# Two linear-attention blocks on one core: the turned strip of G goes by GpSimd's queue, and the kv products stand later

## The chip, the cores and the metric

The kernel runs on one core of a Trainium2 chip, as one program. Its engines each run an in-order queue: TensorE (PE) multiplies, VectorE (DVE) and ScalarE (ACT) do the elementwise work and empty PSUM, GpSimd (POOL) and SyncE (SP) issue DMAs. The metric is device time in microseconds: 573.85 us for the kernel before, the median of three runs (573.29 to 576.09).

## The reference

Two independent linear-attention blocks, A and B, each with its own x (1, 2048, 640), wqkv (640, 1920) and wo (640, 640), all float32; their outputs stand side by side in a (1, 2048, 1280) result. Per block, with 32 heads of 20:

```
q, k, v = split(x @ wqkv)                       # 32 heads x 20
phi(t)  = where(t > 0, t + 1, exp(t)) + 1e-6
kv  = sum over s of phi(k)[s] v[s]^T            # 20 x 20 per head
z   = sum over s of phi(k)[s]
o   = phi(q) kv / (phi(q) . z + 1e-6)
out = concat over heads(o) @ wo
```

## The kernel before

**Algebra.** The kernel never forms v. It sums G = X^T phi(K), a 640 x 640 matrix, over the rows of x, and gets kv = Wv^T G per head. kv is then multiplied with wo into a matrix M (640 x 640) that takes phi(q) straight to the output. Block A is "block one" (b=0), block B "block two" (b=1). Nearly every product is written as three matmuls of a high and a low part (names ending in h and l; DVE makes the low part by a subtraction, ACT the high part by a copy).

**Stages.** First come the k products and G of both blocks, then the q and o stages. Rows go in pairs of 128-row tiles (`kpair`, NPB = 8 pairs per block); a pair has seven k steps, each of 6 or 9 matmuls of 320 columns into a PSUM bank ka, kb or ke (L316). Into the steps of a pair `fill` puts other work: parts of G of the rows before (`gsteps`, L544; psg for 512 direct columns), and in pair NPB+1 block one's kv products (`kvmm`, L603).

**The turned strip.** G lives in one tile, `gall`, called gacc in the profile: 128 partitions x 5 x 640. Its columns 0 to 511 are computed directly. Its last 128 columns are computed transposed, as psr, and added into `gall[:, :, 512:]` (L557). When the sum is complete `gback` turns them: DVE transposes blocks of 32 x 32 into a tile gt (L579), four DMAs write it to DRAM as rd (L583; each 32 partitions x 20 pieces of 128 bytes, 80 KB), and one DMA reads the whole strip back into gall (L586; 320 KB, 640 pieces of 512 bytes). Before this read lands no kv product may start, since each reads all of G. This happens twice, once per block; both use gall.

**What sets the order.** Everything up to the start of the q stage is noted in a plan and emitted by a list scheduler: each job has an engine, a cost, a due time worked back from its users, and `dma` gives the share of the wire that it is taken to need. `safe` makes the planner count a DMA's result as later by up to so much, `late` sets how far behind PE's place a job without users may be due. PE's order is that of the notes; ACT, DVE, POOL and SP take what is due first, and SP has at most eight DMAs in flight in the plan. The queues that result are fixed in the program.

The q and o stages are written out by hand: a step ("q", u, c, k) is three matmuls of 512 columns into psq (L980 to L982), five of them (k = 0 to 4) for one of five column tiles c of a row group u; `at(slot, f, ...)` hangs further work on a slot, and `run(slot)` issues it. At the slot's place each f issues its whole work on all engines. So for block two `kvmm2` issues one group's kv products (L1040; ten matmul records), the mask on DVE (kvt, L1044) and the copy kvh on ACT; the subtraction kvl follows at the next slot. `load_o` loads wo (L1030), `split_o` splits it (woh on ACT, L974; wol on DVE, L971), `mmm2` multiplies kv and wo into psm. There are six groups of heads, four of six heads and two of four. kv uses the two PSUM banks tagged "e", and mmm2 takes one of these as well, so a third kv product waits until DVE has taken the first from its bank. `load_xraw` (L1011) loads the next group's rows of x, xql (L932) their stored low parts. After each column tile ACT computes eq and rq from psq (L1151, L1152) and DVE pq and acc (L1153, L1163).

**SP's queue** holds nearly all loads, the xd stores, and the rd and gacc transfers of the strip. **GpSimd's queue** holds the zacc transfers (sums of phi(k), L407), the small zd and zq transfers (L652, L654), and later stores.

Of the kernel before, what the change touches and what calls it, by code (L numbers as in the profile page):

```python
# [77 lines left out]
class Plan:  # L78
# [9 lines left out]
    def note(self, engine, n, fn, w, r, ahead=None, dma=None, late=None, by=None, due=None, safe=0.0, lat=0.0):  # L88
        base = self.RATE.get(engine)
        j = Job(engine, base[0] + base[1] * n if base else n, fn, ahead, dma)  # L90
        for part, writes in [(p, True) for p in w] + [(p, False) for p in r]:
            sp = part.space
            if sp.where is not None and sp not in j.spaces:
                j.spaces.append(sp)
            for lo, hi, other, wrote in sp.uses:
                if lo < part.hi and part.lo < hi and (writes or wrote) and other is not j:
                    j.deps.add(other)
            if writes:
                sp.uses = [u for u in sp.uses if not (part.lo <= u[0] and u[1] <= part.hi and u[2] is not j)]
            sp.uses.append((part.lo, part.hi, j, writes))  # L100
        for d in j.deps:
            d.nexts.append(j)
        for sp in j.spaces:
            sp.left += 1
        if engine == "PE":
            j.ideal = self.pe_at
            self.pe_at += j.cost
        j.late = self.pe_at + (25.0 if late is None else late)
        if by is not None:
            j.late = self.pe_at + by  # L110
        j.by, j.set, j.safe, j.lat = by, due, safe, (LAT if due is None else 1.9) + lat
        self.jobs.append(j)
        return j
# [105 lines left out]
def tile_linear_attn_pair(ctx: ExitStack, tc: tile.TileContext, ins, out: bass.AP):  # L219
    nc = tc.nc  # L220
    P = 128
# [3 lines left out]
    NG = NT // 4  # L225
# [5 lines left out]
    NPB = NT // 2  # L231
# [34 lines left out]
    gall = base.tile([P, NC, D], F32, name="gacc", tag="gacc", bufs=1)  # L266
# [15 lines left out]
    note = plan.note  # L282
# [29 lines left out]
    def mms(terms, o, start):  # L312
        n = len(terms)
        for k, ((ah, al), (wh, wl)) in enumerate(terms):
            for i, (a, w) in enumerate(((ah, wh), (ah, wl), (al, wh))):
                nc.tensor.matmul(o, a.r, w.r, start=start and k == i == 0,  # L316
                                 stop=k == n - 1 and i == 2, skip_group_check=True)
# [21 lines left out]
    rd = [dram.tile([D, P], F32, name=f"rd{b}") for b in range(NB)]  # L339
# [61 lines left out]
    def pk_split(hi, lo, p, n):  # L401
        note("ACT", n + 110, lambda: act(hi.r, p.f, AF.Identity, bias=epst), [hi], [p, K0.all], by=8.0)  # L402
        note("DVE", n, lambda: stt(lo.r, p.f, EPS, hi.f, op0=OP.add, op1=OP.subtract), [lo], [p, hi], by=9.0)  # L403
# [5 lines left out]
    def z_open(b):  # L409
        zac[b] = [Space("zacc", D, (GD,)) for _ in range(2)]  # L410

    def pk_space():
        return Space("pkh", D, GRP, F32R), Space("pkl", D, GRP, F32R)
# [53 lines left out]
    def kpair(p, fill):  # L467

        b = p // NPB
        first = p % NPB == 0  # L470
        if first:
            z_open(b)
        terms = kterms(kleft(p), wf[b])
        T = [Space("kt", D, ANY) for _ in range(2)]
        E = [Space("ek", D, ANY) for _ in range(2)]
        hl = [pk_space() for _ in range(2)]

        def step(n):
            tm, k, start = terms[n]
            rd = [x for a, w in tm for x in (*a, *w)]  # L480

            def products():
                o = BK[k].open(("ka", "ke", "kb")[k]) if start else BK[k].tile
                mms(tm, o[:, :HF], start)

            note("PE", MM * 3 * len(tm), products, [BK[k].all], rd)

        def copy(h, t, k):
            o = T[t][h * HF:h * HF + HF]
            note("ACT", HF, lambda: act(o.f, BK[k].tile[:, :HF], AF.Copy), [o], [BK[k].all])  # L490

        def plus(h, t, k):
            o = T[t][h * HF:h * HF + HF]
            note("DVE", HF, lambda: tt(o.f, BK[k].tile[:, :HF], o.f, op=OP.add), [o], [BK[k].all, o])

        def finish(n):
            e, t = E[n].all, T[n].all
            note("ACT", D, lambda: act(e.f, t.f, AF.Exp), [e], [t], by=6.0)
            note("ACT", D, lambda: act(t.f, t.f, AF.Relu), [t], [t], by=6.0)  # L499
            note("DVE", D, lambda: stt(e.f, e.f, 1.0, t.f, op0=OP.min, op1=OP.add), [e], [e, t], by=7.0)  # L500
            pk_split(hl[n][0].all, hl[n][1].all, e, D)
            z_add(first, zac[b][n].all, e)

        after = {0: [(copy, 0, 0, 0)], 2: [(copy, 1, 0, 0)], 3: [(plus, 0, 0, 2)], 4: [(copy, 1, 1, 0), (plus, 1, 1, 1)],
                 5: [(copy, 0, 1, 0), (finish, 1)], 6: [(plus, 1, 0, 1), (finish, 0)]}
        for n in range(7):
            step(n)
            for f, *a in after.get(n, ()):
                f(*a)
            for f, *a in fill.get(n, ()):  # L510
                f(*a)
        for t in range(2):
            pks[2 * p + t] = hl[t]
# [3 lines left out]
    WD = 4 * P  # L517
# [44 lines left out]
    def gsteps(i, s, alone=False):  # L562
        if s == 0:
            x, y, u = gset(i, True, 0, 2), gset(i, True, 2, 3), gset(i, False, 0)
            v = gset(i, False, 1, k=6 if alone else None)
            if alone:
                back = [(gback, i // NG)] if i % NG == NG - 1 else []
                return {0: [x[0], y[0], u[0], v[0], *x[1:], *y[1:], *u[1:], *back, *v[1:]]}
            out = {1: [x[0], y[0]], 3: [*x[1:], *y[1:]], 4: u, 5: [v[0]], 6: v[1:]}
        else:  # L570
            x, y, z = (gset(i, False, c) for c in (2, 3, 4))
            out = {1: [x[0]], 3: x[1:], 4: y, 5: [z[0]], 6: z[1:]}
        return out

    def gback(b):

        t = Space("gt32", D, ANY)
        turned = [G[b, c][WD:D] for c in range(NC)]
        note("DVE", D, lambda: nc.vector.transpose(t.all.f, gall[:, :, WD:]), [t.all], turned)  # L579
        rows = rd[b].rearrange("(j r) n -> r j n", r=32)  # L580
        v = Space("rd", 4)
        for q in range(4):
            note("SP", 0.07, lambda q=q: nc.sync.dma_start(  # L583
                rows[:, :, 32 * q:32 * q + 32], t.all.f[32 * q:32 * q + 32].rearrange("r (j s) -> r j s", s=32)),
                [v[q:q + 1]], [t.all], dma=0.6)
        note("SP", 0.07, lambda: nc.sync.dma_start(gall[:, :, WD:], rd[b].rearrange("(c p) n -> p c n", p=P)),  # L586
             turned, [v.all], dma=1.0, safe=6.0)

    kvt = {}

# [248 lines left out]
    def filled(i, s, late=False):  # L839
        fill = {}  # L840
        for n, x in gsteps(i, s).items():
            fill.setdefault(LATER[n] if late else n, []).extend(x)
        return fill
# [13 lines left out]
    gready(NG - 1)  # L857
    whole(NG - 1, 0)
    wf[1] = forms("wk", ins[1]["wk"], w_split)
    kpair(NPB, filled(NG - 1, 1))  # L860
    place = ((1, 6, 0, 6), (2, 0, 1, 6), (2, 2, 2, 6), (3, 0, 3, 6), (3, 2, 4, 6), (4, 0, 5, 6))
    kvs = {3: [(kvmm, g, (6, 7, 3)[g]) for g in range(3)], 4: [(kvmm, g, (4, 5, 6)[g - 3]) for g in range(3, 6)]}
    for p in range(NPB + 1, NP):
        if p == NPB + 1:
            fl = kvs
# [120 lines left out]
    def at(slot, f, *a):  # L986
        todo.setdefault(slot, []).append((f, a))
# [371 lines left out]

    for g in range(NGR):  # L1360
        at(("q", 0, 0, 0), load_o, 1, g)
        at(("q", 0, (0, 1, 1, 2, 2, 3)[g], (2, 0, 3, 0, 3, 0)[g]), kvmm2, 1, g)
        at(("q", 0, 1 + g, 1) if g < 4 else ("q", 1, 0, 2 * g - 7), split_o, 1, g)
        at((("q", 0, 2, 2), ("q", 0, 3, 2), ("q", 0, 4, 4), ("q", 0, 4, 4), ("q", 1, 1, 2), ("q", 1, 2, 2))[g], mmm2, 1, g)
        at((("q", 0, 2, 4), ("q", 0, 3, 4), ("q", 1, 0, 1), ("q", 1, 0, 3), ("q", 1, 1, 4), ("q", 1, 2, 4))[g],
           store_m, nc.gpsimd)

# [19 lines left out]
        at(("o", h - 1, 2 * c + 1), split_w, "q", 1, c)  # L1387

    for c in range(NC):
        at(("q", 0, (0, 0, 1, 1, 2)[c], (1, 4, 1, 4, 1)[c]), load_xraw, 1, c)  # L1390
        at(("q", 0, 4, c - 1) if c else ("q", 0, 3, 3), load_xq, 1, c)
        at(("q", 0, 4, c) if c else ("q", 0, 3, 4), round_xq, 1, c)
        for u in range(1, NU - 1):
            at(("q", u, 3, c), load_xraw, u + 1, c)
            at(("q", u, 4, c), load_xq, u + 1, c)
            at(("o", u - 1, 9 if (u, c) == (1, 2) else 2 * c + 4), round_xq, u + 1, c)
# [94 lines left out]
```

## Time and profile before

| what | value |
|---|---|
| time, median of three runs | 573.85 us (573.29 to 576.09) |
| the profiled execution's own time | 573.23 us |
| its span (first to last instruction) | 571.5 us |
| granted TensorE clock, mean | 0.997 |
| busy PE / DVE / ACT / POOL | 561.5 / 427.4 / 361.8 / 62.9 us |
| DMA | 118.92 MB, mean 208 GB/s over the span |

A wait is read as "engine, what, line <- releaser, tensor: us in total, times, longest". A row of the timeline gives start, length, engine, line, operation, output <- inputs, sizes and, in square brackets, the idle time of the engine before it and who ended it. On SP and POOL the length of a DMA row is the time that the engine needed to issue it; the list of DMAs gives the time from issue to landing. In rows of stretches stand the stretch, its length, then the busy time and count of PE, PEld, DVE, ACT and POOL, the granted clock, the share of the 16 DMA engines and GB/s.

### The profile page before, as it was taken

How to read it: one execution, taken by the hardware profiler on the slowest of the kernel's cores; microseconds unless marked ns; L12 is line 12 of the kernel's file. 1: busy time of each engine (PE TensorE's matmuls, PEld its weight loads, DVE VectorE, ACT ScalarE, POOL GpSimd, SP SyncE). 2: the span in 40 equal slices, each digit the busy share in tenths (PEclk: the TensorE clock that was granted, in tenths of full speed). 3: DMA queues.
4: the chain of work that ended last, by engine and by line, in shares of the span. 5: the costliest groups of instructions: out<-in, count | busy, mean ns of one | idle time of the engine just before them, and what ended most of it. 6: DMA issues, size and time to landing. Idle time of an engine off the chain costs nothing.

```text
span 571.5 us, 8956 instructions
## 1 busy us (share of the span) xinstructions
PE 561.5 (98%) x3224; PEld 512.3 (90%) x3224; DVE 427.4 (75%) x689; ACT 361.8 (63%) x668; POOL 62.9 (11%) x103
## 2 busy tenths in 40 slices
PE   9999999999999999999979999999999999999997
PEld 7998999988899999998858889898989989898997
DVE  7788687589888668987635799967788685767791
ACT  6777466574768757767225768675767656665551
POOL 0210011110011021111010102210012201001010
PEclk9999999999999999999989999999999999999999
DMA  8993755949939677798998994764273997122022
GB/s 307 379 256 116 201 146 138 269 102 280 295 100 249 189 194 214 209 288 230 276 326 281 324 322 150 257 229 137 90 256 110 340 392 272 47 75 92 1 93 92
DMA packets 74879, 118.92 MB, mean 208 GB/s; under 512 B 12084, under 2 KB 36692, under 8 KB 74836
## 3 DMA queue, kind: packets, MB, share of 16 engines
q1 hardware_dynamic: 65620, 91.05, 49.4%
q0 software_dynamic: 8928, 26.92, 16.9%
q8 instruction: 25, 0.41, 0.3%
q10 hardware_dynamic: 288, 0.39, 0.2%
q14 instruction: 18, 0.15, 0.1%
HBM read 71.78 MB, written 36.07 MB: 189 GB/s over the span
## 4 chain that ended last, share of the span: by engine, by line
PE 94%; DMA 2%; DVE 1%; SPq 1%; ACT 0%; issue 0%
PE psg L544 16%; PE pa L1293 12%; PE ka L316 9%; PE psq L980 8%; PE psq L982 8%; PE psq L981 8%; PE pe L1293 6%; PE psr L544 5%; PE ke L316 5%; PE psk L778 4%; PE psb L1293 4%; PE kb L316 3%; DMA gacc<-rd 2%; PE pskv L1040 1%; PE pskv L603 1%; PE psm L630 1%
## 5 line engine op out<-in xcount | busy, mean ns | idle before, releaser
L981 PE MATMUL psq<-xql,wh 128*128 128x512 f32 x200 | 78.2, 391 | 0.6 <-DMA xql<-xd 0.6
L980 PE MATMUL psq<-xqh,wh 128*128 128x512 f32 x200 | 78.7, 394 | 0.0
L982 PE MATMUL psq<-xqh,wl 128*128 128x512 f32 x200 | 78.2, 391 | 0.0
L544 PE MATMUL psg<-pkh,xnl 128*128 128x512 f32 x160 | 63.0, 394 | 0.0
L544 PE MATMUL psg<-pkl,xnh 128*128 128x512 f32 x160 | 62.8, 393 | 0.0
L544 PE MATMUL psg<-pkh,xnh 128*128 128x512 f32 x160 | 62.3, 389 | 0.0
L490 ACT ACTIVATE kt<-ka 128x320 f32<-128x320 f32 x52 | 22.7, 436 | 58.3 <-PE ka L316 58.0
L407 POOL DMA_DIRECT2D zacc<-ek x32 | 26.6, 830 | 229.8 <-DVE ek L500 168.0
L1153 DVE SCALAR_TENSOR_TENSOR pq<-eq,rq 128x512 f32<-128x512 f32 x40 | 27.6, 691 | 31.4 <-ACT rq L1152 31.3
L1151 ACT ACTIVATE eq<-psq 128x512 f32<-128x512 f32 x40 | 23.9, 597 | 37.5 <-PE psq L982 35.2
L981 PEld LDWEIGHTS psq<-xql,wh 128*128 128x128 f32 x200 | 37.7, 189 | 8.3 <-DMA xql<-xd 1.1
L982 PEld LDWEIGHTS psq<-xqh,wl 128*128 128x128 f32 x200 | 37.7, 188 | 8.0
L1308 ACT ACTIVATE o<-pa 128x320 f32<-128x320 f32 x64 | 27.9, 437 | 26.5 <-PE pa L1293 26.0
L980 PEld LDWEIGHTS psq<-xqh,wh 128*128 128x128 f32 x200 | 37.9, 189 | 7.2
L544 PEld LDWEIGHTS psg<-pkh,xnl 128*128 128x128 f32 x160 | 30.0, 188 | 6.4
L544 PEld LDWEIGHTS psg<-pkl,xnh 128*128 128x128 f32 x160 | 30.0, 188 | 4.9
L544 PEld LDWEIGHTS psg<-pkh,xnh 128*128 128x128 f32 x160 | 30.1, 188 | 4.7
L500 DVE SCALAR_TENSOR_TENSOR ek<-ek,kt 128x640 f32<-128x640 f32 x26 | 21.4, 822 | 15.9 <-ACT kt L499 15.9
L557 DVE TENSOR_TENSOR gacc<-psg,gacc 128x512 f32<-128x512 f32 x30 | 20.4, 689 | 13.3 <-PE psg L544 13.0
L402 ACT ACTIVATE pkh<-ek,epst 128x640 fp32r<-128x640 f32 x32 | 26.5, 829 | 5.6 <-DVE ek L500 4.7
L403 DVE SCALAR_TENSOR_TENSOR pkl<-ek,pkh 128x640 fp32r<-128x640 f32 x32 | 26.2, 820 | 1.4 <-ACT pkh L402 1.4
L1293 PE MATMUL pa<-fm,dah 128*128 128x320 f32 x112 | 26.2, 309 | 0.0
(237 smaller groups left out, 1668.6 us busy)
## 6 DMA issues: line engine op xcount, KB each, us to landing
zacc<-ek POOLq DMA_DIRECT2D x32, 320.0 KB, 5.0
xql<-xd SPq DMA_DIRECT2D x40, 256.0 KB, 4.8
xd<-xl SPq DMA_DIRECT2D x29, 320.0 KB, 5.1
out<-o POOLq DMA_DIRECT2D x28, 320.0 KB, 4.0
xns<-in_A_x SPq DMA_DIRECT2D x16, 320.0 KB, 5.1
xts<-in_B_xt_tiles SPq DMA_DIRECT2D x16, 320.0 KB, 4.8
xns<-in_B_x SPq DMA_DIRECT2D x16, 320.0 KB, 6.2
xqs<-in_A_xt SPq DMA_DIRECT2D x20, 256.0 KB, 5.5
```

The costliest lines, as they stand in the source:

```text
L316: nc.tensor.matmul(o, a.r, w.r, start=start and k == i == 0, stop=k == n - 1 and i == 2, skip_group_check=True)
L402: note("ACT", n + 110, lambda: act(hi.r, p.f, AF.Identity, bias=epst), [hi], [p, K0.all], by=8.0)
L403: note("DVE", n, lambda: stt(lo.r, p.f, EPS, hi.f, op0=OP.add, op1=OP.subtract), [lo], [p, hi], by=9.0)
L407: note("POOL", 1.0, lambda: nc.gpsimd.dma_start(z.f, p.f, **kw), [z], [p], dma=1.0 if first else 1.86)
L544: nc.tensor.matmul(o[:, :n], a.r, w.r, start=j == 0 and q == 0, stop=j == 2 and q == 2, skip_group_check=True)
L980: nc.tensor.matmul(o, whi, xhi, start=first, stop=False)
L981: nc.tensor.matmul(o, whi, xlo, start=False, stop=False)
L982: nc.tensor.matmul(o, wlo, xhi, start=False, stop=last)
L1151: nc.scalar.activation(e, ps, AF.Exp)
L1153: nc.vector.scalar_tensor_tensor(pq[u][:, c, :], e, 1.0, r, op0=OP.min, op1=OP.add)
L1293: nc.tensor.matmul(ps, x, y, start=start and n == i == 0, stop=n == len(terms) - 1 and i == 2, skip_group_check=True)
L1308: copy = lambda x, y: nc.scalar.activation(x, y, AF.Copy)
```

## The change

Three edits. In `gback` the four writes and the read of the strip are issued by GpSimd instead of SP, and their costs in the plan are other ones (each 1.0 of POOL's time; 0.3 instead of 0.6 of the wire for a write; `late=8.0` in place of `safe=6.0` on the read). Around the border of the blocks, a part of G that filled pair NPB moves: products of steps 4 and 5 go to step 5 and to steps 1 and 2 of the next pair, and block one's kv products go from steps 3 and 4 of that pair to 4 and 5. In the q stage block two's kv products stand up to six q steps further on (the first behind nine steps instead of three), with two of the mmm products and four of the u=1 loads of x moved as well; the slots of `split_o` are the same.

```diff
--- before.py
+++ after.py
@@ -580,11 +580,11 @@
         rows = rd[b].rearrange("(j r) n -> r j n", r=32)
         v = Space("rd", 4)
         for q in range(4):
-            note("SP", 0.07, lambda q=q: nc.sync.dma_start(
+            note("POOL", 1.0, lambda q=q: nc.gpsimd.dma_start(
                 rows[:, :, 32 * q:32 * q + 32], t.all.f[32 * q:32 * q + 32].rearrange("r (j s) -> r j s", s=32)),
-                [v[q:q + 1]], [t.all], dma=0.6)
-        note("SP", 0.07, lambda: nc.sync.dma_start(gall[:, :, WD:], rd[b].rearrange("(c p) n -> p c n", p=P)),
-             turned, [v.all], dma=1.0, safe=6.0)
+                [v[q:q + 1]], [t.all], dma=0.3)
+        note("POOL", 1.0, lambda: nc.gpsimd.dma_start(gall[:, :, WD:], rd[b].rearrange("(c p) n -> p c n", p=P)),
+             turned, [v.all], dma=1.0, late=8.0)
 
     kvt = {}
 
@@ -857,9 +857,11 @@
     gready(NG - 1)
     whole(NG - 1, 0)
     wf[1] = forms("wk", ins[1]["wk"], w_split)
-    kpair(NPB, filled(NG - 1, 1))
+    last = gsteps(NG - 1, 1)
+    kpair(NPB, {1: last[1], 3: last[3], 5: last[4]})
     place = ((1, 6, 0, 6), (2, 0, 1, 6), (2, 2, 2, 6), (3, 0, 3, 6), (3, 2, 4, 6), (4, 0, 5, 6))
-    kvs = {3: [(kvmm, g, (6, 7, 3)[g]) for g in range(3)], 4: [(kvmm, g, (4, 5, 6)[g - 3]) for g in range(3, 6)]}
+    kvs = {1: last[5], 2: last[6], 4: [(kvmm, g, (6, 7, 3)[g]) for g in range(3)],
+           5: [(kvmm, g, (4, 5, 6)[g - 3]) for g in range(3, 6)]}
     for p in range(NPB + 1, NP):
         if p == NPB + 1:
             fl = kvs
@@ -1359,9 +1361,9 @@
 
     for g in range(NGR):
         at(("q", 0, 0, 0), load_o, 1, g)
-        at(("q", 0, (0, 1, 1, 2, 2, 3)[g], (2, 0, 3, 0, 3, 0)[g]), kvmm2, 1, g)
+        at(("q", 0, (1, 2, 2, 2, 3, 3)[g], (3, 0, 2, 4, 1, 3)[g]), kvmm2, 1, g)
         at(("q", 0, 1 + g, 1) if g < 4 else ("q", 1, 0, 2 * g - 7), split_o, 1, g)
-        at((("q", 0, 2, 2), ("q", 0, 3, 2), ("q", 0, 4, 4), ("q", 0, 4, 4), ("q", 1, 1, 2), ("q", 1, 2, 2))[g], mmm2, 1, g)
+        at((("q", 0, 2, 4), ("q", 0, 3, 4), ("q", 0, 4, 4), ("q", 0, 4, 4), ("q", 1, 1, 2), ("q", 1, 2, 2))[g], mmm2, 1, g)
         at((("q", 0, 2, 4), ("q", 0, 3, 4), ("q", 1, 0, 1), ("q", 1, 0, 3), ("q", 1, 1, 4), ("q", 1, 2, 4))[g],
            store_m, nc.gpsimd)
 
@@ -1387,7 +1389,7 @@
         at(("o", h - 1, 2 * c + 1), split_w, "q", 1, c)
 
     for c in range(NC):
-        at(("q", 0, (0, 0, 1, 1, 2)[c], (1, 4, 1, 4, 1)[c]), load_xraw, 1, c)
+        at(("q", 0, (0, 1, 2, 2, 3)[c], (1, 4, 1, 3, 0)[c]), load_xraw, 1, c)
         at(("q", 0, 4, c - 1) if c else ("q", 0, 3, 3), load_xq, 1, c)
         at(("q", 0, 4, c) if c else ("q", 0, 3, 4), round_xq, 1, c)
         for u in range(1, NU - 1):
```

**GpSimd's queue.** A piece of the difference, whole program up to the small z transfers of block two: zacc is a sum of phi(k), rd the strip's copy in DRAM, gacc the tile of G.

```order
-L407 DMA zacc<-ek 128x640 x22
+L407 DMA zacc<-ek 128x640 x16
+L583 DMA rd_95<-gt_1728 32x20x32 x4
+L407 DMA zacc<-ek 128x640
+L586 DMA gacc<-rd_95 128x5x128
+L407 DMA zacc<-ek 128x640 x5
 L652 DMA zd_93<-zp 128x20
 L407 DMA zacc<-ek 128x640
 L654 DMA zq<-zd_93 32x4x5 x4
 L407 DMA zacc<-ek 128x640 x9
+L583 DMA rd_96<-gt_3335 32x20x32 x4
+L586 DMA gacc<-rd_96 128x5x128
```

Both strips now go through this queue; in block one a zacc transfer stands between the writes and the read.

**PE at block one's kv products** (pskv), in pair NPB+1. Before:

```order
L316 MATMUL kb<-wkh,xh 128x320
L316 MATMUL kb<-wkl,xh 128x320
L316 MATMUL kb<-wkh,xl 128x320
L603 MATMUL pskv<-gacc,wv 120x120 x15
L316 MATMUL ka<-wkh,xsh 128x320
```

And with the change:

```order
L316 MATMUL ka<-wkh,xsh 128x320
L316 MATMUL ka<-wkl,xsh 128x320
L316 MATMUL ka<-wkh,xsl 128x320
L316 MATMUL ka<-wkh,xh 128x320
L316 MATMUL ka<-wkl,xh 128x320
L316 MATMUL ka<-wkh,xl 128x320
L603 MATMUL pskv<-gacc,wv 120x120 x15
```

The nine ka matmuls of the step that stood behind the first kv products stand ahead of them. In pair NPB, twelve psg matmuls that stood between two steps into bank ka stand behind the second.

**DVE at the start of the q stage**, from the end of the z sums on: kvt and kvl are the mask and the split of a kv group, wol the split of a wo group, pq and acc belong to the q steps. Before:

```order
L648 TENSOR_REDUCE zp<-zturn 128x5x4
L1044 TENSOR_TENSOR kvt<-pskv,mask_74 120x120
L971 TENSOR_TENSOR kvl<-kvt,kvh 120x120
L1153 SCALAR_TENSOR_TENSOR pq<-eq,rq 128x512
L1044 TENSOR_TENSOR kvt<-pskv,mask_74 120x120
L971 TENSOR_TENSOR kvl<-kvt,kvh 120x120
L971 TENSOR_TENSOR wol<-wo,woh 120x640
L1044 TENSOR_TENSOR kvt<-pskv,mask_74 120x120
```

And with the change (its lines are two further on):

```order
L648 TENSOR_REDUCE zp<-zturn 128x5x4
L1155 SCALAR_TENSOR_TENSOR pq<-eq,rq 128x512
L973 TENSOR_TENSOR wol<-wo,woh 120x640
L1046 TENSOR_TENSOR kvt<-pskv,mask_74 120x120
L973 TENSOR_TENSOR kvl<-kvt,kvh 120x120
L1155 SCALAR_TENSOR_TENSOR pq<-eq,rq 128x512
L1165 SCALAR_TENSOR_TENSOR acc<-pq,z,acc 128x512
L1046 TENSOR_TENSOR kvt<-pskv,mask_74 120x120
L973 TENSOR_TENSOR kvl<-kvt,kvh 120x120
L973 TENSOR_TENSOR wol<-wo,woh 120x640
L1046 TENSOR_TENSOR kvt<-pskv,mask_74 120x120
```

The first split of wo stood behind two kv groups and stands ahead of the first; on ACT the copies woh and kvh stand in the same order.

## The prediction

> **What bounds the kernel now.** I read the page first, then the waits of PE, then the chain, then PE's timeline at the two places the waits name.
>
> ```profile
> PE 561.5 (98%) x3224; PEld 512.3 (90%) x3224; DVE 427.4 (75%) x689; ACT 361.8 (63%) x668; POOL 62.9 (11%) x103
> PE pskv L1040 <- DMA gacc<-rd: 3.4, 1, 3.4
> PE pskv L603 <- DMA gacc<-rd: 1.0, 1, 1.0
> PE psq L981 <- DMA xql<-xd: 0.6, 1, 0.6
> ```
>
> TensorE is busy for 561.5 of 571.5 us, so a change that neither adds nor removes a matmul can win only PE's idle time. Apart from one row at the start of the program, these are all the waits of PE that the view lists: both kv products wait for the strip of G to come back, 3.4 and 1.0 us.
>
> ```profile
> 139.38 1.33 PE ka L316 x9
> 147.33 6.72 DMA gacc<-rd
> 157.50 1.32 PE ka L316 x9
> 165.74 0.88 PE psm L630 x6
> 286.03 6.19 DMA gacc<-rd
> ```
>
> The chain (start, length) goes through both reads of the strip: they land at 154.05 and 292.22, and PE starts at once.
>
> ```profile
> 152.77 0.31 PE L316 MATMUL kb<-wkh,xl 128*128 128x320 f32 x1
> 285.72 0.39 PE L980 MATMUL psq<-xqh,wh 128*128 128x512 f32 x1
> 286.42 0.40 PE L980 MATMUL psq<-xqh,wh 128*128 128x512 f32 x1
> 288.14 0.50 PE L981 MATMUL psq<-xql,wh 128*128 128x512 f32 x1 [0.65 <-DMA xql<-xd]
> 292.31 2.33 PE L1040 MATMUL pskv<-gacc,wv 128*120 128x120 f32 x10 [3.43 <-DMA gacc<-rd]
> 294.30 0.77 PE L980 MATMUL psq<-xqh,wh 128*128 128x512 f32 x1
> 295.72 0.40 PE L980 MATMUL psq<-xqh,wh 128*128 128x512 f32 x1
> 297.10 1.21 PE L1040 MATMUL pskv<-gacc,wv 128*120 128x120 f32 x10
> 298.07 0.48 PE L980 MATMUL psq<-xqh,wh 128*128 128x512 f32 x1
> ...
> 292.00:294.00 2.00, 1.69 (x8) 1.72 (x9) 0.00 (x0) 0.00 (x0) 0.00 (x0) 0.57 1.04 364
> 294.00:296.00 2.00, 2.00 (x9) 1.68 (x8) 0.57 (x2) 0.30 (x1) 0.91 (x2) 0.58 1.07 294
> ```
>
> In the last two rows (PE, PEld, DVE, ACT, POOL, then granted clock) the clock is 0.57 and 0.58 behind the 3.43 us gap. That gap therefore costs more than itself. The first kv group runs from 292.31 to 294.30, 1.99 us; the next needs 298.07-297.10=0.97. The q step behind it takes 295.72-294.30=1.42 instead of 286.42-285.72=0.70. Together 1.74 us. Block two thus pays 0.65+3.43+1.74=5.8, block one 1.0: 6.8 us is the most that can be won here.
>
> In a sentence beside it: the Trainium skill ("TensorE: Matmul & The Clock Gate", Part 1) puts the drop to half clock behind an idle window of about 3.4 us, and about 3.4 us to return; the 3.43 us gap with its two windows agrees. By that rule several short waits of the same sum would keep the full clock.
>
> **Block one.** Removed: the 1.0 us wait. Added on PE: with the psg products moved away, two k steps that write the same ka bank stand back to back, so the second waits for ACT's copy out of that bank, which nothing now covers (before, twelve psg matmuls did). The kv products stand one k step later. On DVE the add into the strip and its transpose fall behind the three wkl subtractions.
>
> ```profile
> 136.75 0.84 DVE L579 STREAM_TRANSPOSE gt<-gacc 128x640 f32<-128x640 f32 x1
> 138.36 0.49 DVE L310 TENSOR_TENSOR wkl<-d,wkh 128x320 fp32r<-128x320 f32 x1
> 140.74 0.44 ACT L490 ACTIVATE kt<-ka 128x320 f32<-128x320 f32 x1 [1.89 <-PE ka L316]
> 138.19 6.03 SPq L583 DMA_DIRECT2D rd<-gt  x4
> rd<-gt SPq DMA_DIRECT2D x4, 80.0 KB, 7.0
> L407 POOL DMA_DIRECT2D zacc<-ek x32 | 26.6, 830 | 229.8 <-DVE ek L500 168.0 <-PE psg L544 23.1 <-DVE ek L795 21.0
> 295.09 2.22 POOL L654 DMA_DIRECT2D zq<-zd  x4 [5.13 <-DMA zd<-zp]
> ```
>
> The eviction: the step's ka ends at 139.38+1.33=140.71, ACT's copy at 141.18: 0.5, with the signal 0.6 us (0.5 to 0.8).
>
> When the strip lands: the last wkl ends at 138.85, the transpose at 139.7, two microseconds later than now (137.6). Then GpSimd issues the four writes, p us each, the last lands up to 7.0 us after its issue, and the read takes 6.7 plus (p-0.6) more, since the same engine issues it: 139.7+3p+7.0+0.1+6.7+(p-0.6)=152.9+4p. No row shows a GpSimd issue of 640 pieces. From below, the four small zq cost 2.22/4=0.55 each; from above, paying each 128 rows anew makes 5x0.55=2.75. Plain and accumulating zacc, which differ in work, have a mean of 0.83, so the cost is mostly fixed; I take p=0.7, nearest to the low row. The strip then lands at 155.7.
>
> When it is needed: kb ends at 153.08, plus the eviction 0.6 and the k step now ahead, 1.32: 155.0. The new wait is 0.7; it is 0 if the writes take less than 7.0, which they did in block two (4.6, below). One zacc transfer stands between the writes and the read in GpSimd's queue, and whoever delays that delays the read: its ek is computed earlier in the new order, so I give it 0.2. The moved psg groups cost nothing themselves, they are the same matmuls, and the last one's add into G has two k steps, 2.6 us, ahead of kv. What queues on GpSimd behind the waiting read are more zacc transfers, which nothing reads before the end of the pairs, and in block two the small zd and zq, whose zp comes later than the read. I take 0.4 (0 at p=0.55; 2.3 at p=1.1; 8.9 at p=2.75). Block one: -1.0+0.6+0.4=0.0.
>
> **Block two.** The strip's road is the same, but q steps cover it.
>
> ```profile
> 275.58 0.85 DVE L579 STREAM_TRANSPOSE gt<-gacc 128x640 f32<-128x640 f32 x1
> 278.12 4.32 SPq L583 DMA_DIRECT2D rd<-gt  x4
> rd<-gt SPq DMA_DIRECT2D x4, 80.0 KB, 4.6
> 282.00:284.00 2.00, 2.00 (x11) 1.65 (x10) 0.69 (x1) 0.00 (x0) 0.00 (x0) 1.00 0.63 116
> 284.00:286.00 2.00, 2.00 (x11) 1.64 (x10) 0.08 (x1) 0.00 (x0) 0.00 (x0) 1.00 0.69 100
> 290.45 0.36 SPq L1030 DMA_DIRECT2D wo<-in_B_wo  x1
> wo<-in_B_wo SPq DMA_DIRECT2D x1, 300.0 KB, 6.9
> 299.37 0.72 ACT L974 ACTIVATE woh<-wo 120x640 fp32r<-120x640 f32 x1
> 300.12 0.83 DVE L971 TENSOR_TENSOR wol<-wo,woh 120x640 fp32r<-120x640 f32 x1 [0.35 <-ACT woh L974]
> 301.48 0.28 DVE L1044 TENSOR_TENSOR kvt<-pskv,mask 120x120 f32<-120x120 f32 x1 [0.53 <-PE pskv L1040]
> 304.76 0.28 DVE L1044 TENSOR_TENSOR kvt<-pskv,mask 120x120 f32<-120x120 f32 x1
> 305.40 0.28 DVE L971 TENSOR_TENSOR kvl<-kvt,kvh 120x120 fp32r<-120x120 f32 x1 [0.37 <-ACT kvh L974]
> ```
>
> The transposed strip is there at 276.4, one more wl ahead of it (0.7) makes 277.1; plus 3p=2.1, 4.6 to 7.0, and 6.2+0.2: it lands at 290.2 to 292.6. The first kv group now stands behind nine q steps: 285.72+9x0.69=291.9, later with any wait for xql. So the strip no longer binds, or by half a microsecond.
>
> What is late next is wo. Its weight split (split_o) kept its slots while kv moved six steps, so ACT's woh and DVE's wol for group 0 now stand **ahead** of the mask and split of the first kv group. The first wo lands at 290.45+6.9=297.4. The queue ahead of it has to move the same bytes; SP is no longer held 4.32 us by the rd issues, and the DMA share of 0.63 and 0.69 in those four microseconds shows how much work could move up: 2x0.37+2x0.31=1.4. So 296.0 to 297.4. From there: woh to wol 0.75 (299.37 to 300.12), wol about 0.75, then from one kvt to the next with kvh, eq, rq, pq and acc between, 3.3 (301.48 to 304.76), kvl of that group 0.64+0.28, the second wol 0.75, and the third kvt 0.35: 6.8. Only this third kvt frees the PSUM bank of the fourth kv group, whose PE start is thus 302.8 to 304.2. Unhindered it would be 285.72+15x0.69+3x0.97+0.9 (one mmm)=299.9. The loss is 2.9 to 4.3; I take **3.7**, the later side, because the shares on both sides of the hole are above 1.0 and the loads of xqs moved forward fill part of it. Any xql wait lies inside this, since the end of the chain is set by the clock of wo. It is spread over three or four stops (xql, second and third kv group's kvt, fourth kv) of less than 2 us, so I charge no clock loss.
>
> ```profile
> xqs<-in_A_xt SPq DMA_DIRECT2D x20, 256.0 KB, 5.5
> ```
>
> Four of the u=1 xqs loads go back by four or five q steps and are charged nothing: each is rounded nine to eleven steps after its issue, 6.2 us or more of q steps and the kv and mmm groups between, against 5.5 to land. If that cover were gone, PE would stand at the first step of u=1 for the rest, about 1 us.
>
> **Sum** against the profiled run's own 573.23: block one 0.0, block two 3.7-5.8=-2.1, together -2.1, that is 571.1. The median of the runs shown, 573.85, lies 0.6 above that run, so I forecast **571.7**.
>
> **Rivals.** (A) *The wo chain does not bind.* If SP, freed, brings wo four microseconds earlier, only xql's 0.65 is left: 0.0+0.65-5.8=-5.2, median 568.7. For it: 4.32 us of held SP; against it: shares around 1.0 on all other slices, so earlier issues only queue.
>
> (B) *GpSimd is the slow road; the other side.* If it pays per piece, p=1.8 (midway), the strip lands at 160.1 in block one, a 5.1 us gap that also halves the clock (1.7), and in block two at 277.1+5.4+7.0+7.4=296.9, a stop of 5.0 with 1.7 of clock: (-1.0+0.6+5.1+1.7)+(6.7-5.8)=+7.3, median 581. It decides from w=2.1 more in block one, p above 1.1. Against it: every GpSimd row is near 0.55 to 0.83. For it: no row has 128-byte pieces from that engine.
>
> (C) *The queue brings nothing, only kv's place does.* Strip and wo land as late as now, plus the two microseconds of the later transpose: 154.05+2.1=156.15 in block one, a wait of 1.15; 297.4 for wo, 4.3: (-1.0+0.6+1.15)+(4.3-5.8)=-0.75, median 573.1. The Trainium skill ("DMA: Bandwidth & Descriptors", Issuing engines are not separate DMA queues) says that DMAs of all engines interleave on the same 16 DMA engines and that another issuer saves only the sequencer's issue time; that speaks for C. The trace bears it out so far: shares above 1.0 with one queue.
>
> **How the numbers follow.** Main case 0.43 (median 569.8 to 573.2), A 0.20 (567 to 570), C 0.22 (572.3 to 574.5), B 0.15, of which half stays under 577. A measurement of this kernel can tell about 0.5%, 2.9 us, so faster begins below 571.0. Faster: A 0.20 and 0.16 of the main case, 0.36. Slower: above 576.7, 0.12 of B. The rest, 0.52, is no change. Range 567.8 to 576.5.
>
> **What would show it.** Right: no wait of pskv for gacc in block two, no clock below 1.00 around 292, waits of pskv or psm for DVE's kvt around 300 to 304, ka waiting once for ACT at about 141; POOL's rd issues of 0.6 to 0.9. Wrong: rd issues above 1.1 us; a pskv wait on gacc over 2 us; a first wo that lands before 294; a wait later in the q stage that the rows here don't have.

## The result and the profile after

The changed kernel takes 570.09 us, median of six runs (569.27 to 571.38), against 573.57 for the kernel before: a ratio of 0.9936, 95% interval 0.9914 to 0.9958. In a second comparison one of the six executions, the profiled one, took 929.84 us at a mean granted clock of 0.558; the other five have a median of 570.50 and a ratio of 0.9934 (0.9910 to 0.9958). It is faster by 0.6%, 3.5 us; forecast were 571.7 and a range of 567.8 to 576.5. Every ratio below is against the kernel before, run beside it on the same chip.

The page of the profiled execution (569.27, span 567.5) and all waits of PE that the view lists, after the change:

```profile
PE 559.6 (99%) x3224; PEld 510.5 (90%) x3224; DVE 426.4 (75%) x689; ACT 362.6 (64%) x668; POOL 70.0 (12%) x113
PE pskv L1042 <- DVE kvt L1046: 2.8, 2, 1.5
PE psi L692 <- DVE ones L324: 1.0, 1, 1.0
PE ka L316 <- ACT kt L490: 0.5, 1, 0.5
PE psq L983 <- DMA xql<-xd: 0.2, 1, 0.2
```

Both waits for the strip of G are gone. In their place stand two waits of kv products for DVE's kvt and one of ka for ACT's copy. PE's busy time fell from 561.5 to 559.6: the same 3224 matmuls, so these 1.9 us are the matmuls' own time; about 1.7 of them are the half clock of the kernel before (0.57 and 0.58 in two rows of 2 us in the prediction). The listed waits fell from 6.0 (3.4+1.0+0.6+1.0) to 4.5. That is 3.4 of the 4.0 us by which the span is shorter; the other 0.6 lies behind PE's last matmul: the span went on for 3.95 us after it before (from 567.55) and for 3.26 with the change (from 564.24). The forecast has no term for this, and no run shows where it comes from.

The strip's road on GpSimd, from POOL's timeline (length is the time to issue):

```profile
139.46 2.80 POOL L583 DMA_DIRECT2D rd<-gt  x4 [13.41 <-DVE xsr L459]
148.82 0.86 POOL L586 DMA_DIRECT2D gacc<-rd  x1 [2.12 <-DMA rd<-gt]
276.25 2.79 POOL L583 DMA_DIRECT2D rd<-gt  x4 [9.61 <-DVE gt L579]
284.13 0.87 POOL L586 DMA_DIRECT2D gacc<-rd  x1 [5.09 <-DMA rd<-gt]
DMA to landing us min/median/max: 4.8/5.1/5.4
```

The last row is the list of the two reads of gacc. One issue costs 2.80/4=0.70 us. The reads land at about 153.6 (148.82+4.8) and 289.5 (284.13+5.4).

PE's timeline at the places of the prediction, and the granted clock there (the third column from the right):

```profile
141.07 0.41 PE L316 MATMUL ka<-wkh,xh 128*128 128x320 f32 x1 [0.53 <-ACT kt L490]
154.62 3.31 PE L603 MATMUL pskv<-gacc,wv 128*120 128x120 f32 x30
284.90 0.39 PE L982 MATMUL psq<-xqh,wh 128*128 128x512 f32 x1
291.07 1.21 PE L1042 MATMUL pskv<-gacc,wv 128*120 128x120 f32 x10
292.04 0.48 PE L982 MATMUL psq<-xqh,wh 128*128 128x512 f32 x1
292.83 0.40 PE L982 MATMUL psq<-xqh,wh 128*128 128x512 f32 x1
297.59 1.31 PE L1042 MATMUL pskv<-gacc,wv 128*120 128x120 f32 x10 [1.46 <-DVE kvt L1046]
302.61 1.31 PE L1042 MATMUL pskv<-gacc,wv 128*120 128x120 f32 x10 [1.31 <-DVE kvt L1046]
...
292.00:294.00 2.00, 2.00 (x14) 1.73 (x13) 0.00 (x0) 0.00 (x0) 0.00 (x0) 1.00 1.04 248
296.00:298.00 2.00, 0.54 (x5) 0.41 (x4) 1.11 (x3) 0.92 (x3) 1.59 (x3) 1.00 1.04 274
```

The first kv products of both blocks start with no wait. The third and the fourth group of block two wait, and the clock stays at 1.00 through both. Why they wait stands in the timelines of ACT and DVE at the same place:

```profile
295.75 0.74 ACT L976 ACTIVATE woh<-wo 120x640 fp32r<-120x640 f32 x1 [4.54 <-DMA wo<-in_B_wo]
...
296.52 0.82 DVE L973 TENSOR_TENSOR wol<-wo,woh 120x640 fp32r<-120x640 f32 x1 [6.16 <-ACT woh L976]
297.26 0.28 DVE L1046 TENSOR_TENSOR kvt<-pskv,mask 120x120 f32<-120x120 f32 x1
...
301.54 0.82 DVE L973 TENSOR_TENSOR wol<-wo,woh 120x640 fp32r<-120x640 f32 x1 [0.34 <-ACT woh L976]
302.28 0.28 DVE L1046 TENSOR_TENSOR kvt<-pskv,mask 120x120 f32<-120x120 f32 x1
```

The first kv group is ready from 292.3 on, yet its mask stands at 297.26, behind a wol that waits 6.16 us for woh, which waits for wo. The third group needs the bank that this mask empties.

### The profile page after: what moved, and what is told of

It is laid out like the page before. It is cut to its first block, busy times and chain, and to the rows that moved or that the text cites. A ratio compares the mean times of both kernels' runs of the same rounds, so it can differ in the third digit from the quotient of the medians.

```text
span 567.5 us, 8954 instructions
## 1 busy us (share of the span) xinstructions
PE 559.6 (99%) x3224; PEld 510.5 (90%) x3224; DVE 426.4 (75%) x689; ACT 362.6 (64%) x668; POOL 70.0 (12%) x113
## 4 chain that ended last, share of the span: by engine, by line
PE 94%; DMA 3%; DVE 1%; ACT 1%; SPq 0%; issue 0%; ACTq 0%
PE psg L544 19%; PE pa L1295 12%; PE ka L316 10%; PE psq L983 7%; PE psq L984 7%; PE psq L982 7%; PE pe L1295 6%; PE ke L316 5%; PE psr L544 5%; PE psk L778 4%; PE psb L1295 4%; PE kb L316 3%; DMA wo<-in_B_wo 1%; DMA xql<-xd 1%; PE pskv L603 1%; PE psm L630 1%
```

## The experiments

My theory was the forecast's: block two's kv place takes away the 3.43 us wait with its clock loss and pays with the wo chain; the queue matters where the strip would else be late. The main rivals: the queue alone does it, the queue brings nothing, and the kvt waits have nothing to do with wo.

### The queue alone

```diff
 (gback of the kernel before, nothing else)
-            note("SP", 0.07, lambda q=q: nc.sync.dma_start(
+            note("POOL", 1.0, lambda q=q: nc.gpsimd.dma_start(
...
-        note("SP", 0.07, lambda: nc.sync.dma_start(gall[:, :, WD:], ...
+        note("POOL", 1.0, lambda: nc.gpsimd.dma_start(gall[:, :, WD:], ...
```

> The kernel before with the strip's writes and reads on GpSimd's queue (and their costs in the plan) and nothing else; all kv products stand where they stood. Theory 1 (the queue itself brings something, since SP no longer holds the transfers up): with 0.7 us per issue the strip of block one lands near 137.6+2.8+5.5+5.2=151, ahead of its kv products at 153.1, so the 1.0 us wait is gone; in block two it lands near 276.4+2.8+5.2+5.4=289.8 instead of 292.2, the wait falls from 3.43 to about 1.8 us and the clock stays at 1.00, which saves 1.0+1.6+1.7=4.3: about 569.3 against 573.6. Theory 2 (all issuers share the same DMA engines, so the strip lands when it did): waits of 1.0 and 3.4 stay, the clock falls to about 0.57 behind the second, 573 to 574.

Measured: 572.13, ratio 0.9971 (0.9955 to 0.9986). Waits of PE, the read's issue, and stretches of the run:

```profile
PE pskv L1040 <- DMA gacc<-rd: 3.8, 1, 3.8
...
284.80 0.88 POOL L586 DMA_DIRECT2D gacc<-rd  x1 [6.05 <-PE psg L544]
...
288.00:290.00 2.00, 0.00 (x0) 0.00 (x0) 0.45 (x1) 0.00 (x0) 0.59 (x1) 0.93 0.94 310
290.00:292.00 2.00, 0.84 (x4) 0.88 (x5) 0.00 (x0) 0.00 (x0) 0.00 (x0) 0.50 0.98 346
292.00:294.00 2.00, 2.00 (x10) 1.90 (x9) 0.28 (x1) 0.17 (x1) 0.00 (x0) 0.50 1.02 272
294.00:296.00 2.00, 2.00 (x6) 1.52 (x6) 0.28 (x1) 0.14 (x1) 0.80 (x2) 0.50 1.00 241
296.00:298.00 2.00, 2.00 (x15) 1.81 (x14) 0.69 (x1) 1.09 (x3) 1.40 (x3) 0.87 1.04 269
```

In block one the wait is gone, as theory 1 had it. In the profiles of all four runs that have this queue without block one's edit (this one and three below) no kv product of block one waits for the strip: there the queue alone is enough.

In block two both theories were wrong in part. The strip came sooner, 291.1 instead of 292.2, but PE was there 1.5 us sooner as well, since block one's wait and the 0.65 us wait for xql were gone. The wait grew to 3.8 us, and the half clock lasted about twice as long as in the kernel before (6.8 us against 3.4, worked out in the last section). So in this execution the earlier strip brought block two nothing: from the first q step to the first matmul into pa (the start of the o stage), which is the same work in both, PE took 52.53 us against 52.15 before. What the run shows of a gain lies elsewhere: PE reaches the q stage 0.63 us earlier (285.09), and the span ends 3.60 instead of 3.95 us after PE's last matmul. The edit also changes the costs of these DMAs in the plan, and with them places of loads in SP's queue; no run separates the plan from the queue.

### Block two's places alone

```diff
 (the kernel before, strip on SP; the three lines of the q stage as in the change)
-        at(("q", 0, (0, 1, 1, 2, 2, 3)[g], (2, 0, 3, 0, 3, 0)[g]), kvmm2, 1, g)
+        at(("q", 0, (1, 2, 2, 2, 3, 3)[g], (3, 0, 2, 4, 1, 3)[g]), kvmm2, 1, g)
```

> The kernel before with block two's kv products, two mmm and four x loads moved as in the change, the strip still on SP, block one as before. Theory 1 (place and queue each bring part): the strip lands at 292.2 as before, the first kv group now stands at 285.7+9x0.69=291.9 or a little later, so the 3.43 us wait and the halved clock (together 5.2) go; two or three waits of kv for the mask (kvt) behind the wo split come, 2.8 to 3.7 us; xql's 0.65 stays; block one keeps its 1.0: 573.6-5.2+3.2=571.6. Theory 2 (the gain is the queue's alone): 573 to 574.

Measured: 571.76, ratio 0.9965 (0.9951 to 0.9979).

```profile
PE psq L981 <- DMA xql<-xd: 2.3, 2, 1.3
PE pskv L1040 <- DVE kvt L1044: 1.3, 1, 1.3
PE pskv L603 <- DMA gacc<-rd: 0.3, 1, 0.3
```

The time is theory 1's to 0.2 us, but that is in part luck, since what remains is put together otherwise: 2.3 for xql and 1.3 for kvt, not 0.65 and 3. With the strip on SP the later xql loads are issued from 282.88 on (with the change from 279.79), and whatever PE waits for them it does not wait for wo afterwards, since the end of that chain is set by wo's landing. The wait for gacc and the half clock are gone with the place alone. Block one's wait was 0.3 here and 1.0 in the kernel before: it differs by 0.7 us between two executions with the same block one.

### Block two's places put back

```diff
 (the changed kernel)
-        at(("q", 0, (1, 2, 2, 2, 3, 3)[g], (3, 0, 2, 4, 1, 3)[g]), kvmm2, 1, g)
+        at(("q", 0, (0, 1, 1, 2, 2, 3)[g], (2, 0, 3, 0, 3, 0)[g]), kvmm2, 1, g)
 (and the mmm2 and load_xraw lines likewise)
```

> The changed kernel with block two's kv products, mmm and x loads put back to their old places (the first kv group behind three q steps). The strip lands near 289.5 and its kv products want it at 284.9+3x0.69=287.0, so PE waits about 2.6 us there; no kvt wait behind wo, since the first kv groups stand ahead of the wo split. Theory 1 (a gap of 2.6 us does not lower the clock): 570.1+2.6-2.8=569.9. Theory 2 (it does, as behind the 3.43 us): 1.7 more, 571.6. If the wo split binds in any place, kvt waits of 2 us or more show here too and the time is above 572.

Measured: 572.98, ratio 0.9994 (0.9981 to 1.0007): of the changed kernel's gain nothing is left.

```profile
PE pskv L1042 <- DMA gacc<-rd: 5.0, 1, 5.0
...
292.00:294.00 2.00, 1.66 (x8) 1.69 (x9) 0.00 (x0) 0.00 (x0) 0.00 (x0) 0.50 1.06 283
294.00:296.00 2.00, 2.00 (x8) 1.71 (x7) 0.57 (x2) 0.30 (x1) 0.00 (x0) 0.50 1.02 232
```

The expected gap of 2.6 was 5.0 in this execution, since the strip landed at 292.3, no earlier than in the kernel before, so the run does not decide what a gap of 2.6 us does to the clock. It does show that no kvt wait of 2 us comes with the old places, and that with block one's edit in place the whole gain hangs on the q stage's edit. The queue alone took 572.13 on the same chip; whether the 0.85 us between the two are block one's edit or only the longer wait is not shown.

### Block one's edit alone

```diff
 (the kernel before, strip on SP)
-    kpair(NPB, filled(NG - 1, 1))
+    last = gsteps(NG - 1, 1)
+    kpair(NPB, {1: last[1], 3: last[3], 5: last[4]})
 (and kvs of the next pair as in the change)
```

> The kernel before with block one's edit alone (the moved parts of G, its kv products one step later), the strip on SP, block two as before. Theory 1 (the step gives the cover, the queue is not needed in block one): the 1.0 us wait goes, the ka wait of 0.5 comes: 573.4-0.5=572.9; block two keeps its 3.4 us wait with the halved clock. Theory 2 (the transpose comes two microseconds later, so without the queue the strip is late by more than the k step covers): a wait of pskv L603 of 0.5 to 1.2 us stays beside the 0.5, 573.5 to 574.5.

Measured: 573.94, ratio 1.0012 (0.9991 to 1.0034).

```profile
PE pskv L603 <- DMA gacc<-rd: 1.0, 1, 1.0
PE ka L316 <- ACT kt L490: 0.5, 1, 0.5
```

Theory 2: the wait stays at 1.0 although the kv products stand one k step later, because the strip, turned later, lands two microseconds later (PE's kv products start at 156.41), and the 0.5 for the ka bank comes on top.

### All but block one's edit

```diff
 (the changed kernel)
-    last = gsteps(NG - 1, 1)
-    kpair(NPB, {1: last[1], 3: last[3], 5: last[4]})
+    kpair(NPB, filled(NG - 1, 1))
 (and kvs as in the kernel before)
```

> The changed kernel with block one's fill and kv places as before the change (queue and block two's part kept, wo splits where they were). Theory 1 (in block one the queue alone does it): no wait of pskv L603 for gacc, no ka wait, PE is 0.5 to 0.8 us ahead of the changed kernel behind block one; the kvt waits of block two stay: 569.4. Theory 2 (being earlier in block two only meets the loads of xql, which do not come earlier): the 0.5 to 0.8 us turn up again as a longer xql wait, of 1 to 2.4 us, and the time is that of the changed kernel or worse by the clock, 570 to 571.5.

Measured: 570.63, ratio 0.9932 (0.9908 to 0.9955); the changed kernel beside it on the same chip 570.50. That is no difference that these runs can tell. Of that second run of the changed kernel was expected:

> The changed kernel itself, beside the next three on one chip, so that they can be compared with it directly. 570.1 if the first comparison holds: two kvt waits of 1.3 to 1.5 us, a ka wait of 0.5, no wait for gacc.

The time is as expected. No profile shows its waits at a clock of 1.00, since the one taken is of the execution with 929.84 us.

The waits of the run without block one's edit, and one stretch of it:

```profile
PE pskv L1040 <- DVE kvt L1044: 2.3, 2, 1.3
PE psq L981 <- DMA xql<-xd: 1.9, 1, 1.9
...
290.00:292.00 2.00, 1.92 (x8) 1.61 (x9) 0.00 (x0) 1.09 (x2) 0.00 (x0) 1.00 1.03 335
```

There is no ka wait and no wait for block one's strip, so in block one the queue alone does it. But theory 2 also holds: what PE is ahead there it meets again as a wait of 1.9 us for xql, where the changed kernel had 0.2. Block one's edit costs PE about half a microsecond and brings nothing that these runs show, and taking it out alone brings nothing either.

### The wo split behind the kv groups

```diff
 (the changed kernel)
-        at(("q", 0, 1 + g, 1) if g < 4 else ("q", 1, 0, 2 * g - 7), split_o, 1, g)
+        at(("q", 0, (2, 3, 3, 4)[g], (3, 0, 4, 1)[g]) if g < 4 else ("q", 1, 0, 2 * g - 7), split_o, 1, g)
```

> The changed kernel with the splits of wo groups 0 to 3 hung on later slots (steps (2,3), (3,0), (3,4), (4,1) instead of (1,1), (2,1), (3,1), (4,1)), so that mask and split of the first three kv groups stand ahead of them on ACT and DVE. Theory 1 (the two kvt waits of 1.46 and 1.31 us come from woh standing ahead of kvh until wo lands at 295.7): both go; the first mmm then needs woh and wol at 295.7+1.6=297.3 and stands at about 298.5, so nothing takes their place: 570.1-2.8=567.3. Theory 2 (the kv groups stand too close for two PSUM banks, whatever wo does): pskv still waits 2 us or more for kvt, 569.5 to 570.5.

Measured: 569.28, ratio 0.9928 (0.9913 to 0.9943).

```profile
PE psm L983 <- DVE wol L973: 1.8, 2, 1.3
```

Both kvt waits are gone, so they came from the order of woh and kvh, as theory 1 says and theory 2 denies. The expected 2.8 us are not won, though, since another wait takes 1.8 of them: the mmm products of groups 0 and 2 now wait for their wol (0.45 and 1.30). I had placed the splits too late. From the first q step to the first matmul into pa the profile has 48.76 us, against 49.79 in the changed kernel. So the places were moved again:

```diff
 (the changed kernel)
+        at(("q", 0, (2, 3, 3, 4)[g], (2, 0, 2, 0)[g]) if g < 4 else ("q", 1, 0, 2 * g - 7), split_o, 1, g)
```

> The changed kernel with the wo splits of groups 0 to 3 at steps (2,2), (3,0), (3,2), (4,0): one slot earlier for group 0 and two or more for group 2 than in the run with late splits, where wol of these two groups held PE up for 0.45 and 1.30 us. Theory 1 (what is left there is only the place of the two splits): both waits go and no kvt wait comes back, since the masks of the first three kv groups still stand ahead of the second split: PE waits in the q stage under 0.5 us in all, 2.5 us less than in the changed kernel, 567.6. Theory 2 (wo itself lands too late for any place, 295.7 to 299): woh now holds ACT ahead of the third kvh, a wait of 1 us or more shows at pskv or psm, 569 or more.

Measured: 568.17, ratio 0.9902 (0.9884 to 0.9919).

```profile
PE psm L983 <- DVE wol L973: 0.6, 1, 0.6
PE ka L316 <- ACT kt L490: 0.5, 1, 0.5
PE psq L983 <- DMA xql<-xd: 0.5, 1, 0.5
```

No kvt wait is left, and one wol wait of 0.6, now of group 3. Theory 1 holds in the main: of the changed kernel's 2.8 us some 2 are back (the same stretch now takes 47.57 us). PE's waits in the q stage are 1.1 us in all, though, and not under 0.5.

### The first kv group earlier

```diff
 (the changed kernel: five steps ahead of the first kv group, then seven, instead of nine)
+        at(("q", 0, (0, 2, 2, 2, 3, 3)[g], (4, 0, 2, 4, 1, 3)[g]), kvmm2, 1, g)
+        at(("q", 0, (1, 2, 2, 2, 3, 3)[g], (1, 0, 2, 4, 1, 3)[g]), kvmm2, 1, g)
```

> The changed kernel with the first kv group of block two behind five q steps instead of nine, all else as changed. The strip landed at 289.6 to 292 in the runs so far; PE is there at 284.9+5x0.69=288.4, so it waits 1.2 to 3.5 us for gacc. Theory 1 (the clock falls only behind a gap that is near 3.4 us or longer): a gap under 3 us leaves the clock at 1.00; since the first mask then stands ahead of woh, the kvt wait of 1.46 goes and the one of 1.31 stays or shrinks: 570.1+1.5 to 2.5-1.5=570.1 to 571.1. Theory 2 (any gap above 1.5 us halves it): 1.7 more, 572 to 573.

Measured with five steps: 570.55 (single runs from 568.83 to 573.72), ratio 0.9951 (0.9928 to 0.9975).

```profile
291.56 1.51 PE L1042 MATMUL pskv<-gacc,wv 128*120 128x120 f32 x10 [2.26 <-DMA gacc<-rd]
...
290.00:292.00 2.00, 0.43 (x4) 0.47 (x5) 0.00 (x0) 0.00 (x0) 0.00 (x0) 1.00 0.93 283
292.00:294.00 2.00, 2.00 (x12) 1.81 (x11) 0.28 (x1) 0.57 (x2) 0.00 (x0) 0.62 1.07 302
294.00:296.00 2.00, 2.00 (x6) 1.52 (x6) 0.89 (x2) 1.24 (x3) 0.00 (x0) 0.53 1.04 274
```

A gap of 2.26 us was enough for the clock to fall, so theory 1 is wrong on the clock. Theory 2 is right on the clock for this gap and wrong on the time: all kvt waits are gone, not one of the two, with the first mask ahead of woh. The eleven executions fall into three groups by mean clock: 1.00 with 568.83 to 569.60 us, 0.997 with 570.36 to 570.93, 0.994 with 571.98 to 573.72.

> The changed kernel with the first kv group of block two behind seven q steps instead of nine, its mask now just ahead of the first woh on both engines. PE is there at 284.9+7x0.69=289.7, the strip lands between 289.6 and 291.9: a gap of 0 to 2 us. Theory 1 (kvt behind woh is the price of the order): the wait of 1.46 goes, that of 1.31 stays or shrinks to 0.5, as the second mask still stands behind woh: 570.1-1.5+0 to 1=568.6 to 569.6, clock 1.00 if the gap stays under 1.5. Theory 2 (the clock falls whenever one window holds 2 us or more of idle PE): in executions with the late strip 1 to 1.7 us more, a wide spread as with five steps (568.8 to 573.7).

Measured with seven: 568.66, ratio 0.9903 (0.9881 to 0.9926), on the chip where the changed kernel took 570.50.

```profile
PE pskv L1042 <- DVE pq L1155: 1.1, 1, 1.1
PE pskv L1042 <- DVE kvt L1046: 0.2, 1, 0.2
```

This is the wo chain seen from the other side: the split of wo stays where it is, only one mask has passed it, and both kvt waits shrink to 0.2 together. What comes is 1.1 us at the first kv group, at 291.65. The row names DVE's pq, but this pq had ended at 291.05, and the read of the strip was issued at 285.05 and took 6.5 us to land: 291.55, so it was most likely the strip.

### A version that beats both

```diff
 (the kernel before with the queue, block two's places and the wo splits of the run with 568.17)
...
 (and the same with the first loads of xql due earlier)
-        note("SP", 0.07, fetch, [lo.all], [gate.all, xdv[0].all], ahead=12.0, dma=0.8, late=6.0 + c)
+        note("SP", 0.07, fetch, [lo.all], [gate.all, xdv[0].all], ahead=14.0, dma=0.8, late=2.0 + c)
```

> As the run before, but with block one's fill and kv places as in the kernel before (the strip on GpSimd's queue, block two's kv moved, wo splits moved). Theory 1 (block one's moved part of G is not needed once the queue is GpSimd's, and costs the 0.5 us for the ka bank): the strip of block one lands near 152 and its kv products at 153.1 wait for nothing, no ka wait: 0.5 us less than the run before, 567.1. Theory 2 (the part has to move for the strip to be in time): a wait of pskv L603 for gacc of 0.5 to 1 us, 568.

Measured without the earlier loads: 568.43 (567.60 to 570.97), ratio 0.9916 (0.9895 to 0.9936). The profiled execution was the one with 570.97:

```profile
PE psq L981 <- DMA xql<-xd: 2.4, 1, 2.4
...
292.00:294.00 2.00, 2.00 (x6) 1.51 (x6) 0.69 (x1) 0.94 (x2) 0.00 (x0) 0.50 1.06 269
```

Neither of its theories named this: block one needs no edit, as the first said, but the time won there runs into xql, in this execution by 2.43 us and with the half clock. The mean clock was 0.996 in this execution and 1.00 in the other five, which took 567.60 to 568.76.

> The version with the queue, block two's kv places and the moved wo splits, block one as before (568.43), and the plan's due time for the five first xql loads four microseconds earlier, so that SP issues them ahead of the last loads of the form stage. Theory 1 (the spread of 567.6 to 571.0 comes from xql alone, which in the profiled execution held PE up for 2.43 us and halved the clock): no xql wait above 0.5, clock 1.00, wol wait 0.6 stays: 567.0 and a spread under 1.5 us. Theory 2 (the wire is full, what is issued earlier only delays another load): a wait of the same size appears at psq for xqh or at psg, 568 to 570.

Measured: **566.80** (566.03 to 567.13), ratio **0.9870** (0.9848 to 0.9893).

```profile
PE psi L692 <- DVE ones L324: 1.0, 1, 1.0
PE psm L981 <- DVE wol L971: 0.6, 1, 0.6
```

These two rows are all of PE's waits. As theory 1 has it, the spread shrinks from 3.4 to 1.1 us, and no other load took the place of xql. The due time moved by four microseconds, but in the schedule that came of it SP issues the five loads between 259.9 and 276.3 instead of 276.4 and 283.1. Against the changed kernel on the same chip (570.50) it is 3.7 us faster. No run has the earlier loads together with block one's edit, so what leaving that edit out adds here is not shown.

## Why the prediction held, and where its sizes were off

The direction, the places and the new waits were right; the forecast of -2.1 was too small against a measured -3.5, and so the largest chance lay on no measurable change. In the two profiled executions the span is 4.0 us shorter: 0.8 up to the start of the q stage, 2.4 in the q stage, 0.1 behind it and 0.7 after PE's last matmul. The last two are no part of the forecast.

**GpSimd's issue.** Taken as p=0.7 between 0.55 and 2.75; measured 0.70. Rival B, which needed p above 1.1, falls.

**Block one, put at 0.0, was worth 0.8.** PE starts the q stage at 284.90 instead of 285.72; by 0.16 of that it was ahead already in front of the first edit, at 140. The removed wait (1.0) and the new one for the ka bank (0.53, put at 0.6) were right. The term that was mis-sized is the strip's read. The sum had it issued at 139.7+2.1+7.0+0.1=148.9, and it was issued at 148.82; but it took 4.8 us and not 6.8, so the strip landed at 153.6 and not at 155.7, and the kv products, there at 154.62, waited for nothing where I had charged 0.4. How short that read was is partly luck: in the five other profiles with the same block one on this queue it took 4.4 to 6.8 us. My sum also took the edit of block one as part of the gain's price without asking whether the queue needs it. The runs say that it doesn't: the wait is gone with the queue alone, stays at 1.0 with the edit alone.

**Block two, put at -2.1, came to -2.4.** The measure is PE's time from the first q step (285.72 before, 284.90 after) to the first matmul into pa; the 50 q steps between them, all kv groups and the mmm products are the same. The first row is the kernel before, the second the changed one:

```profile
337.87 0.31 PE L1293 MATMUL pa<-fh,dah 128*128 128x320 f32 x1
334.69 0.31 PE L1295 MATMUL pa<-fh,dah 128*128 128x320 f32 x1
```

That is 52.15 and 49.79 us. As forecast, the strip no longer binds (kv at 291.07, strip at about 289.5), though the margin is small: in the nine other profiles with the strip on GpSimd it landed between 289.7 and 293.2. The clock stays at 1.00, and the wo chain binds. From the landing of wo to the fourth kv group the forecast had 6.8 us; measured it is 302.61-295.75=6.9. Counted from the first q step, this group was forecast to start 17.1 to 18.5 us on; it started 302.61-284.90=17.7 on. The stops were forecast as three or four; two came, at the third and the fourth group.

The term that was mis-sized is the reference, 14.2 us for the unhindered path. Without the two waits it is 17.7-1.46-1.31=14.9, in part because a q step behind a kv group takes 292.83-292.04=0.79 instead of 0.70, and because PE starts more slowly behind a wait (the third kv group needs 1.07 us to the next q step, the first 0.97). So PE's listed waits are only 2.96 us (with 0.19 for xql later on) where 3.7 was charged, but the stops cost half a microsecond beyond the listed waits, and 5.8-2.4=3.4 us were given back. The two errors nearly cancel.

**The chances.** "Above 576.7, 0.12 of B" does not fit "B 0.15, of which half stays under 577", which leaves about 0.08 for slower and puts no change at 0.56.

**The wo chain as the cause** was argued from order and durations; moving only the splits, or only one mask past them, took the kvt waits away, and so it is shown. In the three profiles where the first split stands ahead of the first mask, the fourth kv group starts 6.9 us behind the first woh each time (295.75, 297.17 and 297.64 to 302.61, 304.04 and 304.51). That two stops of 1.3 to 1.5 us would cost no clock was right.

**The rivals.** A (wo does not bind) is wrong in its mechanism; 568.7, its time, is about what the kernel takes once the splits are moved (568.17), which is another kernel. C (the queue brings nothing) is wrong too: alone the queue has a ratio of 0.9971, and its interval ends at 0.9986. The places alone have 0.9965, and the two multiply to 0.9936, the ratio of the whole change; so within these intervals the effects add up, as my sum took them. What I had not seen is that the queue alone, in its one profile, brings block two nothing while its kv products stand early.

## To carry to other kernels

When a consumer is moved back in order to hide a transfer, move with it, or look again at, everything that was placed in relation to it on the in-order engines: here a split waiting for a load now stood ahead of the masks and gave back more than half of what block two could win. Measure the parts of a change one by one before crediting any: here the queue and the places each brought about half, and the third part, block one's edit, brought nothing that the runs show. Time won upstream can be lost again at the next load on the path: here that load was xql, and issuing it earlier took the ratio from 0.9916 to 0.9870.

## What the runs showed of the hardware

**The clock fell behind shorter gaps than 3.4 us, and stayed down for 3.4 us or for twice that.** PE waits of 1.46, 1.31 and 1.95 us left it at 1.00; waits of 2.26 and 2.43 us brought it to 0.50. In rows of half a microsecond it fell 2.0 us into the wait of 5.0 and 2.3 us into that of 3.8, but with 2.26 us only 0.9 us after PE had started again.

In the deepest rows the clock is 0.50, so a row of 2 us with the clock c holds 4(1-c) us at half clock. For the gap of 2.26 us the rows give 4x0.38+4x0.47=3.4 us, for the 3.43 us of the kernel before (0.57 and 0.58) also 3.4, for the 3.8 us of the queue alone 4x0.07+6.0+4x0.13=6.8, and for the 5.0 us 6.8 as well. In the run with block one's edit alone a wait of 3.4 us, as in the kernel before, was followed by 6.8. So the price of a gap does not follow from its length alone. The three groups of executions with five steps fit this: at some 570 us, 3.4 us at half clock make a mean of 0.997 and 6.8 us one of 0.994. Counting over fixed stretches of 3.4 us, which begin independently of the program, would explain it; no run tests that. By the Trainium skill ("TensorE: Matmul & The Clock Gate", Part 1) it takes an idle window of about 3.4 us; the 2.26 us here are shorter than that, and the measurement decides.

**More issuers did not make more wire.** The Trainium skill ("DMA: Bandwidth & Descriptors", Issuing engines are not separate DMA queues) says that all run on the same 16 engines. With SP free, the first wo was issued at 287.45 instead of 290.45, three microseconds sooner, and woh could start at 295.75, 8.3 us behind the issue, against 6.9 us to landing before: nearly half of what was gained at the issue was lost again before the landing. That agrees with what the Trainium skill says.
